# PV runs of 12, 10 and 10 units on twelve score buffers in a gated mix of attention and SwiGLU

## The chip, the cores and the metric

The kernel runs on one core of a Trainium2 chip. The metric is device time in microseconds (us). TensorE (PE in the profile) multiplies matrices, ScalarE (ACT) computes the exponentials, VectorE (DVE) and GpSimd (POOL) work on tiles in SBUF, and SyncE (SP) issues the DMAs, one after the other in the order of the program. The kernel is written with a manual schedule: each engine executes its instructions in the order in which the program emits them and waits where an operand is not ready.

## The reference

```python
q, k, v = split(x @ wqkv)                  # S = 2048, D = 512, 32 heads of 16
p = softmax(einsum("bhqd,bhkd->bhqk", q, k) * 16 ** -0.5)
a = einsum("bhqk,bhkd->bhqd", p, v) @ wo
h = silu(x @ w1) * (x @ w3)                # F = 1792
b = h @ w2
g = sigmoid((x * gate_w).sum(-1))
out = g * a + (1 - g) * b
```

All data are float32. The kernel splits the operands of the projections and the FFN in two parts (`hi` and `lo`) and sums three products, to keep the precision.

## The kernel before

After a preamble of some 80 us (transposes of x, the first heads' q and k, v, the gate) one string of tokens, `order`, drives everything else. A **unit** is one block of scores: two heads, 128 keys, 512 queries, so that a step (one pair of heads and one half of the queries) has 32 units, and there are 1024 units in 32 steps. The tokens are:

- **Q**, `score` (L823): one unit's scores, two matmuls on the two halves of the array's rows (L829), and one exp on ScalarE (L833) from PSUM (`S`, two buffers) into one of the score buffers `p` in SBUF.
- **F**, `feed` (L765): one matmul on each half of the rows for work that has nothing to do with the current scores. Two lanes take blocks from `blocks` (L716) in turn: first the q and k projections of the other heads (24 blocks), then the FFN's gate and up products (both `w_product`, L432), then the products of h with w2 (`h_product`, L550), then the output projection. A block of 12 such feeds runs on one half of the rows, then on the other, and its bank `f` (three of them) is then read by VectorE. A new block may take a bank only `REST` = 7 tokens after this.
- **P**, `pv` (L813): the products of two units' exps with V, eight matmuls (L817) that add into `acc`. It frees two score buffers.

Before, `one` has eight units, 21 feeds and one run of four P, and stands 90 times. `two` has eight units, 15 feeds and two runs of two P, and stands 37 times. Eight score buffers, `p0` to `p7`, hold the units between their Q and their P.

What a Q triggers besides: at unit 6 of each step `load_step` (L285) issues 14 DMAs with the next step's `Qt` and `Kt`; deferred work is taken from lists, one item per unit or so: `splits` (GpSimd's halves of weights), `soon` (a gate's exp, at the last Q ahead of a P), `small` (the reciprocals and products of the gates on VectorE, L461 to L481), `loads` (the w2 rows and pieces of h, `halves_of` L508), `stages` (the division by the sums, `divide` L605).

What a finished block triggers (`done`): a q or k block is copied to `gs` (L443), split on GpSimd into `sg` and `gs` (L444, L445) and stored (L187); `gs` and `sg` have two buffers each. A gate is copied (L455), an up product multiplied (L477), and the product with the sigmoid (L481) stored to `h_d` (L482). Pieces of h come back by `load_piece` (L522, load L512), are cast on GpSimd to the high half (L513) and subtracted for the low half (L514). The last P of a step calls `evac` (L795): VectorE copies `acc` to `u` (L799), and SyncE stores it with eight DMAs (L805, L811).

So VectorE, GpSimd and SyncE have a queue of their own in the order of the tokens, and a token that is moved takes what it triggers along.

Of the kernel before, what the change touches and what calls it, by code (L numbers as in the profile page):

```python
# [8 lines left out]
F32 = mybir.dt.float32  # L9
# [8 lines left out]
P = 128  # L18
S = 2048
D = 512  # L20
F = 1792
# [12 lines left out]
def gated_mix_kernel(ctx: ExitStack, tc: tile.TileContext, x, wqkv, wo, w1, w3, w2, gate_w, out):  # L34
# [47 lines left out]
    def slot(tag, dtype=F32R, shape=(P, 512)):  # L82

        return (fw if tag[0] == "f" else fk).tile(list(shape), dtype, name=tag, bufs=BUFS.get(tag, 2))

    def psum2():
        return psum.tile([P, 2, 512], F32, name="S", bufs=2)
# [237 lines left out]
    splits, issued, fed = [], 0, 0  # L325
# [91 lines left out]
    wk = ctx.enter_context(tc.tile_pool(name="wk", bufs=1))  # L417
# [116 lines left out]
    def load_wo(k):  # L534
        if k < 2:
            hi, lo = w2H[3][:, 2 + k, :], w2L[3][:, 2 + k, :]
        else:
            both = wk.tile([P, 2, 512], F32R, name=f"wo{k}")
            hi, lo = both[:, 0, :], both[:, 1, :]
        halves_of(wo[P * k:P * k + P, :], hi, lo, "sg")  # L540
        wo_[k] = hi, lo

    PART = NF
    y_ = {}
# [17 lines left out]
    def h_done(t, part):  # L562
        def done(ps):
            if part == 0:
                y_[t] = wk.tile([P, 512], F32, name=f"y{t % 2}")
                nc.vector.tensor_scalar(y_[t], ps, omg[:, t:t + 1], None, op0=OP.mult)
                return
            y = y_[t]
            nc.vector.scalar_tensor_tensor(y, ps, omg[:, t:t + 1], y, op0=OP.mult, op1=OP.add)
            if part == 1:  # L570
                return
            nc.sync.dma_start(B_d[P * t:P * t + P, :], y)
            if t in (11, 12, 13):
                load_bt(t - 11)
            if t in (4, 5, 6, 7):
                later.append(lambda: load_wo((0, 1, 3, 2)[t - 4]))
            if t == NT - 1:
                stages.append(rest_of_o())
        return done
# [10 lines left out]
    def reciprocals(k, half):  # L590

        rows = lambda d: d[8 * k:8 * k + 8, 1024 * half:1024 * half + 1024].rearrange("h (a t) -> h a t", a=16)
        nc.sync.dma_start(dd, rows(D_d))
        for _ in range(9):
            yield
        nc.vector.reciprocal(dd, dd)
        yield
        nc.sync.dma_start(rows(R_d), dd)

    def fetch_o(k, b, o, r):  # L600
        nc.sync.dma_start(o, O_d[P * k:P * k + P, 512 * b:512 * b + 512])
        src = R_d[8 * k:8 * k + 8, 512 * b:512 * b + 512]
        nc.sync.dma_start(r, bass.AP(tensor=src.tensor, offset=src.offset, ap=[[S, 8], [0, DH], [1, 512]]))

    def divide(k, half):  # L605

        yield from reciprocals(k, half)
        for b in (2 * half, 2 * half + 1):
            for _ in range(5):
                yield  # L610
            if half == 0:
                o, r = slot("hx", F32), slot("gw", F32)
            else:
                both = wk.tile([P, 2, 512], F32, name="od")
                o, r = both[:, 0, :], both[:, 1, :]
            fetch_o(k, b, o, r)
            for _ in range(7):
                yield
            nc.gpsimd.tensor_mul(o, o, r)
            for _ in range(3):  # L620
                yield
            nc.sync.dma_start(N_d[P * k:P * k + P, 512 * b:512 * b + 512], o)
            yield

    bt = {}

    def load_bt(t):
        bt[t] = wk.tile([P, 512], F32, name=f"bt{t % 3}")
        nc.sync.dma_start(bt[t], B_d[P * t:P * t + P, :])

    def o_product(t):
# [25 lines left out]
    def o_done(t):  # L657
        def done(ps):
            mix(t, ps)
            if t < 2:  # L660
                load_ot(t + 6)
            if t < 5:
                load_bt(t + 3)
        return done
# [8 lines left out]
    def rest_of_o():  # L673
        for n, x in zip("HL", (Oh, Ol)):
            for m in range(2):
                both = xp.tile([P, 4, 512], F32R, name=f"x{n}{m}")
                x[2 * m], x[2 * m + 1] = both[:, 0:2, :], both[:, 2:4, :]
        for m, n in enumerate("HL"):
            rows = xp.tile([P, 4, 512], F32, name=f"x{n}2")
            for i in range(4):  # L680
                bt[NT // 2 + 4 * m + i] = rows[:, i, :]
        for k in range(ND - 1):
            for b in (2, 3):
                halves_of(N_d[P * k:P * k + P, 512 * b:512 * b + 512], Oh[k][:, b - 2, :], Ol[k][:, b - 2, :], "fr")
                for _ in range(4):
                    yield
        for t in range(NT // 2, NT):
            nc.sync.dma_start(bt[t], B_d[P * t:P * t + P, :])
            yield
# [105 lines left out]
    def evac(j, half):  # L795
        if half == 1 and j == NPAIR - 1:
            return
        u = wk.tile([P, 512], F32, name="u")
        nc.vector.tensor_copy(u, acc)  # L799
        for gq in range(2):  # L800
            t = 1024 * half + 512 * gq
            for h in range(2):
                r = 32 * (2 * gq + h)
                hh = 2 * j + h
                nc.sync.dma_start(D_d[hh:hh + 1, t:t + 512], u[r + DH:r + DH + 1, :])  # L805
        for gq in range(2):
            t = 1024 * half + 512 * gq
            for h in range(2):
                r = 32 * (2 * gq + h)
                hh = 2 * j + h  # L810
                nc.sync.dma_start(O_d[DH * hh:DH * hh + DH, t:t + 512], u[r:r + DH, :])  # L811

    def pv(two):  # L813
        for j, half, k, gq, n, p in two:
            for h in range(2):
                r = 32 * (2 * gq + h)
                nc.tensor.matmul(acc[r:r + DH + 1, :], V[:, k, 2 * j + h, :], p[:, h, :],  # L817
                                 start=k == 0, stop=k == NT - 1)
            free.append(n)
        if k == NT - 1:  # L820
            evac(j, half)

    def score(j, half, k, gq):  # L823
        i = (NPAIR * half + j) % 2
        ps = psum2()
        t = 512 * gq
        for h in range(2):
            r = 64 * h
            nc.tensor.matmul(ps[:, h, :], Kt[i][r:r + 50, P * k:P * k + P],  # L829
                             Qt[i][r:r + 50, t:t + 512], start=True, stop=True)  # L830
        n = free.pop(0)
        p = wk.tile([P, 2, 512], F32, name=f"p{n}")
        nc.scalar.activation(p, ps, AF.Exp, scale=SCALE)  # L833
        return j, half, k, gq, n, p

# [2 lines left out]


    NP = 8  # L840
    LONG, SHORT = 90, 37
    one = "QQFFFFFF" + "QFFF" * 5 + "QPPPP"
    two = "QFFF" * 5 + "QPPQQPP"
    order = one * LONG + "QQ" + "F" * 7 + two * SHORT + "QFFF" * 5 + "QPPPP"
    free = list(range(NP))

    units = iter([(j, half, k, gq) for half in range(2) for j in range(NPAIR) for k in range(NT) for gq in range(2)])
    pend, clock = [], 0
    for i, c in enumerate(order):
        clock += 1 if c != "P" else 4  # L850
        if c == "Q":
            step = issued // 32 + 1
            if issued % 32 == 6 and step < 2 * NPAIR:
                assert 8 * (ND - 1) - qk_left >= 8 * min(step // 4, ND - 1)
                load_step(step)
            pend.append(score(*next(units)))
            issued += 1
            while splits and splits[0][0] <= issued:
                splits.pop(0)[1]()
            while soon and order[i + 1] == "P":  # L860
                soon.pop(0)()
            if issued % 128 == (40 if issued // 128 == 5 else 12) and 1 <= issued // 128 < 8:
                stages.append(divide((issued // 128 - 1) % 4, (issued // 128 - 1) // 4))
            if issued == 64 * NPAIR - 22:
                stages.append(six_heads())
            if small or later and hurry:
                for _ in range(3 if hurry else 1 + (len(small) > (6 if len(over) < 8 * len(chunks) - 16 else 0))):
                    if small or later and hurry:
                        (small or later).pop(0)()
            if loads and (hurry or issued % 2 or len(over) > 8 * len(chunks) - 12):  # L870
                loads.pop(0)()
            for stage in stages[:1]:
                if next(stage, stages) is stages:
                    stages.pop(0)
        elif c == "F":
            feed()
        else:
            pv(pend[:2])
            pend = pend[2:]
# [20 lines left out]
    k = ND - 1  # L900
# [80 lines left out]
```

## Time and profile before

| | us |
|---|---|
| runs of the kernel | 1403.93, 1404.1, 1404.19 |
| median | 1404.1 |
| the profiled execution | 1403.71 |
| its span in the profile | 1401.9 |
| TensorE busy | 1393.8 |
| ScalarE busy | 1034.3 |
| VectorE busy | 486.9 |
| GpSimd busy | 329.3 |
| mean granted clock | 0.999 |

The span is what the hardware profiler saw from the first instruction to the last; the execution takes 1.8 us more around it. In a row of the timeline stand the start, the duration, the engine, the line of the kernel, the operation, the tiles written and read, and the number of instructions that the row joins; in brackets comes the idle time of the engine before it and what ended it. Rows of TensorE overlap a little, since the next matmul starts while the last one drains. PEld is the loading of weights, which runs beside the matmuls, and SPq is the issuing of DMAs by SyncE.

### The profile page before, as it was taken

The page shows a single profiled execution, that of the slowest core. Times are in us where ns is not written, and L with a number is a line of the kernel's source. Part 1 is how long each engine was busy: PE and PEld are TensorE (multiplying, and loading weights), DVE is VectorE, ACT ScalarE, POOL GpSimd, SP SyncE. Part 2 cuts the span into 40 slices and gives each one's busy share as a digit, 9 for nine tenths or more (in the row PEclk, how much of TensorE's full clock was granted, in tenths as well). Part 3 has the DMA queues.
Part 4 walks back from the last instruction along what each step waited for, and adds up shares of the span by engine and source line. Part 5 has one row for each costly group of instructions (what it writes and reads, how often), then busy time and mean ns, then how long its engine had stood idle before and what let it go on. Part 6 is the DMA issues. An engine that isn't in the chain of part 4 may idle for free.

```text
span 1401.9 us, 29019 instructions
## 1 busy us (share of the span) xinstructions
PE 1393.8 (99%) x11497; PEld 826.4 (59%) x11497; DVE 486.9 (35%) x1083; ACT 1034.3 (74%) x1155; POOL 329.3 (23%) x366
## 2 busy tenths in 40 slices
PE   9999999999999999999999999999999999999998
PEld 8866566566566566566566566566555555555554
DVE  5511111564555546555454554511111101111113
ACT  4457677777777777777777777777677887888784
POOL 6123433011011101110110116432344322212312
PEclk9999999999999999999999999999999999999999
DMA  7653554343223423223333236444354453444632
GB/s 209 166 124 94 133 139 113 73 113 77 46 56 85 114 54 76 69 66 93 74 77 74 66 86 165 118 95 91 87 123 105 105 110 77 111 93 110 157 120 78
DMA packets 112479, 141.03 MB, mean 101 GB/s; under 512 B 16276, under 2 KB 70804, under 8 KB 109264
## 3 DMA queue, kind: packets, MB, share of 16 engines
q1 hardware_dynamic: 111616, 137.92, 41.4%
q8 instruction: 93, 1.52, 0.5%
q10 hardware_dynamic: 720, 1.18, 0.2%
q14 instruction: 50, 0.41, 0.1%
HBM read 90.43 MB, written 48.61 MB: 99 GB/s over the span
## 4 chain that ended last, share of the span: by engine, by line
PE 99%; DVE 0%; issue 0%; DVEq 0%
PE acc L817 33%; PE f L432 27%; PE S L829 19%; PE f L550 11%; PE f L634 2%; PE S L199 2%; PE f L641 1%; PE f L96 1%; PE f L98 1%; PE f L97 1%; PE f L165 0%; PE acc L353 0%; PE f L897 0%; PE S L165 0%; PE S L897 0%; DVE xL L646 0%
## 5 line engine op out<-in xcount | busy, mean ns | idle before, releaser
L833 ACT ACTIVATE p<-S 128x1024 f32<-128x1024 f32 x1024 | 967.9, 1026 | 314.1 <-PE S L829 305.0
L817 PE MATMUL acc<-p,V 128*17 128x512 f32 x4096 | 471.5, 594 | 0.0
L829 PE MATMUL S<-Qt,Kt 50*128 50x512 f32 x2048 | 403.7, 407 | 0.8 <-DVE V L415 0.8
L829 PEld LDWEIGHTS S<-Qt,Kt 50*128 50x128 f32 x2048 | 184.0, 184 | 173.5 <-issue 77.7
L817 PEld LDWEIGHTS acc<-p,V 128*17 128x17 f32 x4096 | 103.4, 97 | 275.2 <-issue 275.2
L463 DVE RECIPROCAL sg<-sg 128x64 f32<-128x64 f32 x448 | 209.2, 517 | 52.7 <-issue 49.1
L432 PE MATMUL f<-xH,fl 64*128 64x512 f32 x1088 | 220.6, 395 | 0.0
L432 PE MATMUL f<-xL,fh 64*128 64x512 f32 x1088 | 219.6, 393 | 0.0
L432 PE MATMUL f<-xH,fh 64*128 64x512 f32 x1088 | 218.0, 389 | 0.0
L328 POOL CAST fh<-fr 128x512 fp32r<-128x512 f32 x34 | 22.4, 658 | 428.0 <-DMA fr<-in_B_w_dram 279.6
L432 PEld LDWEIGHTS f<-xH,fh 64*128 64x128 f32 x1088 | 105.6, 184 | 25.0 <-issue 0.4
L432 PEld LDWEIGHTS f<-xL,fh 64*128 64x128 f32 x1088 | 106.4, 186 | 22.5
L432 PEld LDWEIGHTS f<-xH,fl 64*128 64x128 f32 x1088 | 106.1, 186 | 22.7
L789 DVE MEMSET tick<- 1x1 f32 x198 | 11.7, 59 | 281.2 <-PE f L550 143.0
L455 DVE COPY gs<-f 128x512 f32<-128x512 f32 x56 | 38.5, 688 | 65.5 <-PE f L432 59.3
L461 DVE TENSOR_SCALAR sg<-sg 128x512 f32<-128x512 f32 x56 | 27.3, 488 | 88.0 <-ACT sg L460 84.3
L550 PE MATMUL f<-xH,fh 64*128 64x512 f32 x208 | 57.5, 392 | 0.0
L550 PE MATMUL f<-xH,raw 64*128 64x512 f32 x192 | 57.0, 392 | 0.0
L550 PE MATMUL f<-xL,fh 64*128 64x512 f32 x208 | 56.2, 392 | 0.0
L550 PE MATMUL f<-xH,fl 64*128 64x512 f32 x208 | 55.4, 392 | 0.0
L513 POOL CAST fh<-sg 128x512 fp32r<-128x512 f32 (+1 forms) x32 | 18.0, 563 | 147.3 <-DMA sg<-h_d 91.0
L799 DVE COPY u<-acc 128x512 f32<-128x512 f32 x31 | 21.4, 692 | 86.1 <-PE acc L817 86.1
(202 smaller groups left out, 1324.6 us busy)
## 6 DMA issues: line engine op xcount, KB each, us to landing
Kt<-kH_d SPq DMA_DIRECT2D x128, 128.0 KB
h_d<-sg SPq DMA_DIRECT2D x56, 256.0 KB
sg<-h_d SPq DMA_DIRECT2D x43, 256.0 KB
fr<-in_B_w_dram SPq DMA_DIRECT2D x42, 256.0 KB
Qt<-qH_d SPq DMA_DIRECT2D x128, 64.0 KB
Kt<-kL_d SPq DMA_DIRECT2D x64, 128.0 KB
Qt<-qL_d SPq DMA_DIRECT2D x64, 64.0 KB
b_d<-y SPq DMA_DIRECT2D x16, 256.0 KB
```

The costliest lines, as they stand in the source:

```text
L199: nc.tensor.matmul(ps[:, i, :], w[i][h][:, k, :], xs[b][:, k, :], start=n == 0, stop=n == len(order) - 1)
L328: nc.gpsimd.tensor_copy(hi, src)
L432: return nc.tensor.matmul(ps, w[i == 1][r, k, :], (xL if i == 2 else xH)[b][r, k, :], start=n == 0 and not second, stop=n == 3 * ND - 1 an ...
L455: nc.vector.tensor_copy(gs, ps)
L461: small.append(lambda: nc.vector.tensor_scalar(sg, sg, 1.0, None, op0=OP.add))
L463: small.append(lambda q=q: nc.vector.reciprocal(sg[:, q:q + 64], sg[:, q:q + 64]))
L550: ins = nc.tensor.matmul(ps, hs[t][q][i == 1][r, P * o:P * o + P], (w2L if i == 2 else w2H)[q][r, o, :], start=n == 0 and not second, stop ...
L634: return nc.tensor.matmul(ps, ot[t][i == 1][r, P * k:P * k + P], wo_[k][i == 2][r, :], start=n == 0 and not second, stop=n == 3 * ND - 1 a ...
L799: nc.vector.tensor_copy(u, acc)
L817: nc.tensor.matmul(acc[r:r + DH + 1, :], V[:, k, 2 * j + h, :], p[:, h, :], start=k == 0, stop=k == NT - 1)
L829: nc.tensor.matmul(ps[:, h, :], Kt[i][r:r + 50, P * k:P * k + P], Qt[i][r:r + 50, t:t + 512], start=True, stop=True)
L833: nc.scalar.activation(p, ps, AF.Exp, scale=SCALE)
```

## The change

In the first 16 steps (512 units) the string has, for each step, one run of 12 units and two of 10, in place of four of eight. A run has six feeds after its first two scores and three after each further one up to the last, so a step holds 87 feeds where it had 84. After these come 18 periods of eight units and 45 of the double kind. The numbers of Q, F and P are the same in all; there are 157 runs of P where there were 165.

Twelve units must be held between Q and P. The four further buffers are tiles that are used only later: `od`, `yy` (the two `y` tiles joined in one) and the two halves of a tile `bt` (`b0`, `b1`, called `twin`), which replaces the three `bt` tiles. After 512 units they are not given back to `free`. The last `divide` of the first half reads into `od` where it took `hx` and `gw`.

```diff
     def h_done(t, part):
         def done(ps):
             if part == 0:
-                y_[t] = wk.tile([P, 512], F32, name=f"y{t % 2}")
+                if t == 0:
+                    y_[-1] = wk.tile([P, 2, 512], F32, name="yy")
+                y_[t] = y_[-1][:, t % 2, :]
...
-            if half == 0:
+            if half == 0 and k < 3:
                 o, r = slot("hx", F32), slot("gw", F32)
...
     def load_bt(t):
-        bt[t] = wk.tile([P, 512], F32, name=f"bt{t % 3}")
+        if t == 0:
+            bt[-1] = wk.tile([P, 4, 512], F32, name="bt")
+        bt[t] = bt[-1][:, t % 3, :]
...
-            free.append(n)
+            if type(n) is int or issued < 32 * THIRDS:
+                free.append(n)
...
         n = free.pop(0)
-        p = wk.tile([P, 2, 512], F32, name=f"p{n}")
+        if n in ("b0", "b1"):
+            p = twin[:, 0:2, :] if n == "b0" else twin[:, 2:4, :]
+        else:
+            p = wk.tile([P, 2, 512], F32, name=f"p{n}" if type(n) is int else n)
...
-    LONG, SHORT = 90, 37
-    one = "QQFFFFFF" + "QFFF" * 5 + "QPPPP"
+    THIRDS, LONG, SHORT = 16, 18, 45
+    run = lambda n: "QQFFFFFF" + "QFFF" * (n - 3) + "Q" + "P" * (n // 2)
     two = "QFFF" * 5 + "QPPQQPP"
-    order = one * LONG + "QQ" + "F" * 7 + two * SHORT + "QFFF" * 5 + "QPPPP"
-    free = list(range(NP))
+    order = (run(12) + run(10) * 2) * THIRDS + run(8) * LONG + "QQ" + "F" * 7 + two * SHORT + "QFFF" * 5 + "QPPPP"
+    MORE = ["od", "yy", "b0", "b1"]
+    free = list(range(NP)) + MORE
+    twin = wk.tile([P, 4, 512], F32, name="bt")
```

In the changed kernel the lines from L568 on have other numbers: the score matmuls are L834, PV is L821, the copy of acc L803, its stores L809 and L815.

Three places show what moves. The first is on TensorE at the end of the first step. `xH_157` with `fl` and `fh` of the second weight chunk is the first product of a new q or k block; the P run of unit 32 is `acc<-...`. Before, the rows read:

```order
L829 MATMUL S<-Qt_108,Kt_111 128x512 [waits Activation_49]
L829 MATMUL S<-Qt_108,Kt_111 128x512
L817 MATMUL acc<-p_6190,V 17x512 x2
L817 MATMUL acc<-p_6195,V 17x512 x2
...
L829 MATMUL S<-Qt_109,Kt_112 128x512 [waits PE_49]
L829 MATMUL S<-Qt_109,Kt_112 128x512
L432 MATMUL f<-xH_157,fl_6033 128x512 [waits DVE_49]
L432 MATMUL f<-xH_586,fl_653 128x512
```

After the change, at the same place:

```order
L834 MATMUL S<-Qt_108,Kt_111 128x512 [waits Activation_49]
L834 MATMUL S<-Qt_108,Kt_111 128x512
L432 MATMUL f<-xH_157,fl_6041 128x512 [waits DVE_49,Pool_49]
L432 MATMUL f<-xH_586,fl_653 128x512
L432 MATMUL f<-xL_158,fh_6040 128x512
L432 MATMUL f<-xL_587,fh_652 128x512
L432 MATMUL f<-xH_157,fh_6040 128x512
L432 MATMUL f<-xH_586,fh_652 128x512
L834 MATMUL S<-Qt_108,Kt_111 128x512 [waits Activation_49]
L834 MATMUL S<-Qt_108,Kt_111 128x512
L821 MATMUL acc<-bt,V 17x512 x4
L821 MATMUL acc<-p_6195,V 17x512 x2
```

The matmul that waits for VectorE's copy of a bank stood behind the run of P and stands ahead of it now.

The second place is on VectorE at the end of the fifth step (unit 160), around the copy of acc. Before:

```order
L461 TENSOR_SCALAR sg<-sg 128x512
L463 RECIPROCAL sg<-sg 128x64
L799 COPY u<-acc 128x512
L463 RECIPROCAL sg<-sg 128x64 x3
L477 TENSOR_TENSOR raw<-f,gs 128x512
L463 RECIPROCAL sg<-sg 128x64 x2
L455 COPY gs<-f 128x512
```

After:

```order
L455 COPY gs<-f 128x512
L463 RECIPROCAL sg<-sg 128x64 x3
L803 COPY u<-acc 128x512
L481 TENSOR_TENSOR sg<-raw,sg 128x512
L461 TENSOR_SCALAR sg<-sg 128x512
L463 RECIPROCAL sg<-sg 128x64 x2
L477 TENSOR_TENSOR raw<-f,gs 128x512
L463 RECIPROCAL sg<-sg 128x64 x2
```

Two full-width operations of a gate and two reciprocals now stand between the copy of acc and L477, the operation that reads a bank of TensorE; three reciprocals did before.

The third place is on SyncE, where the FFN ends and the products of h begin. L482 stores h, L512 with `h_d` loads a piece of it, and L277, L270 and L282 are the 14 DMAs of `load_step`. Before, behind those 14:

```order
L282 DMA Qt_108<-m_d 2x1024 x2
L512 DMA fr<-h_d 128x4x128
L482 DMA h_d<-sg 128x512
L512 DMA fr<-h_d 128x2x128
L512 DMA fr<-in_B_w_dram 128x512 x2
L512 DMA sg<-h_d 128x4x128
L482 DMA h_d<-sg 128x512
L512 DMA sg<-h_d 128x4x128
L512 DMA sg<-h_d 128x2x128
L512 DMA sg<-h_d 128x4x128
```

After:

```order
L512 DMA sg<-h_d 128x4x128
L482 DMA h_d<-sg 128x512
L512 DMA sg<-h_d 128x4x128
L277 DMA Qt_108<-qH_d 16x1024
L277 DMA Qt_108<-qL_d 16x1024
...
L270 DMA Kt_111<-kL_d 16x2048
L282 DMA Qt_108<-m_d 2x1024 x2
L512 DMA sg<-h_d 128x4x128
L512 DMA sg<-h_d 128x2x128
L512 DMA sg<-h_d 128x4x128
```

The last store of h and the first load behind it were followed by the further loads of h; the 14 DMAs of a step now lie between.

## The prediction

> **What bounds the kernel now.** I read the page first.
>
> ```profile
> PE 1393.8 (99%) x11497; PEld 826.4 (59%) x11497; DVE 486.9 (35%) x1083; ACT 1034.3 (74%) x1155; POOL 329.3 (23%) x366
> ...
> PE 99%; DVE 0%; issue 0%; DVEq 0%
> PE acc L817 33%; PE f L432 27%; PE S L829 19%; PE f L550 11%; PE f L634 2%; PE S L199 2%; PE f L641 1%; PE f L96 1%; PE f L98 1%; PE f L97 1%; PE f L165 0%; PE acc L353 0%; PE f L897 0%; PE S L165 0%; PE S L897 0%; DVE xL L646 0%
> ...
> L833 ACT ACTIVATE p<-S 128x1024 f32<-128x1024 f32 x1024 | 967.9, 1026 | 314.1 <-PE S L829 305.0
> ```
>
> TensorE is busy for 1393.8 of 1401.9 us and carries 99% of the chain that ended last. So a saving exists only if TensorE's own stream gets shorter, and any wait that TensorE gets is lost in full. The waits of TensorE come next.
>
> ```profile
> PE acc L353 <- DVE acc L349: 1.6, 1, 1.6
> PE S L829 <- DVE V L415: 0.8, 1, 0.8
> ```
>
> Both lie ahead of the token string: the list has no wait in the string itself. Third, the timeline of TensorE over one long period (eight units, one P run) and one short one (eight units, two P runs):
>
> ```profile
> 602.68 3.63 PE L817 MATMUL acc<-p,V 128*17 128x512 f32 x32
> 606.24 0.73 PE L829 MATMUL S<-Qt,Kt 50*128 50x512 f32 x4
> ...
> 608.22 0.40 PE L829 MATMUL S<-Qt,Kt 50*128 50x512 f32 x2
> ...
> 612.86 0.39 PE L829 MATMUL S<-Qt,Kt 50*128 50x512 f32 x2
> 613.18 0.62 PE L817 MATMUL acc<-p,V 128*17 128x512 f32 x4
> ```
>
> ```profile
> 1203.63 1.91 PE L817 MATMUL acc<-p,V 128*17 128x512 f32 x16
> 1205.47 0.73 PE L829 MATMUL S<-Qt,Kt 50*128 50x512 f32 x4
> ...
> 1213.04 0.62 PE L817 MATMUL acc<-p,V 128*17 128x512 f32 x4
> ```
>
> The long period is 613.18 − 602.68 = 10.50 us, the short one 9.41. Between 608.22 and 612.86 lie five groups QFFF: 4.64 / 5 = 0.928 each, so 0.232 for a token Q or F. A run of eight units' PV takes 3.56 (602.68 to 606.24), one of four 1.84: the difference is 0.43 per unit, and 0.12 is left over for the run. A unit in a run of any length n therefore adds 0.928 + 0.43 = 1.358: run(n) = 10.50 + (n − 8) × 1.358.
>
> **The change: the P runs.** The matmuls are the same 1024 Q, 2467 F and 512 P before and after; only the number of P runs changes, 165 to 157. A step of 32 units with its 87 feeds costs 15.93 + 2 × 13.22 = 42.37 us. So the string is 16 × 42.37 + 18 × 10.50 + 45 × 9.42 = 1290.8 against 90 × 10.50 + 37 × 9.42 = 1293.5; with the periods' means over all repeats (10.504 and 9.419) the difference is **−2.9 us**. That is 0.36 for each of eight P runs fewer: the change of direction between Q or F and P, which is all that the change can gain.
>
> Does a run of 12 starve somewhere? ScalarE must deliver an exp for each Q:
>
> ```profile
> 606.84 7.54 ACT L833 ACTIVATE p<-S 128x1024 f32<-128x1024 f32 x8 [1.93 <-PE S L829]
> ```
>
> Eight exps, the last 1.026 long, in 7.54: a pitch of (7.54 − 1.026) / 7 = 0.93, the pitch of QFFF itself. ScalarE follows the scores and does not fall behind with n; I take 0 (bounds 0 to 0.1 per run of 10 or 12, 5 us over 48 runs, if its own pitch were above 0.93). The four new score buffers add no instruction and no DMA. The last divide of the first half writes another tile, with the same instructions: 0.
>
> **The change: what loses its cover.** A P run is also 3.4 to 5.1 us in which VectorE, GpSimd and SyncE catch up while TensorE needs nothing of them. Longer stretches of Q and F lie between P runs now. Three places, by the order of the changed kernel and rows of before.
>
> *The q/k projections (first three steps).* Each finished bank is copied (L443), split on GpSimd and stored; the third copy needs the buffer that the store of the first one frees.
>
> ```profile
> 113.62 0.69 DVE L443 COPY gs<-f 128x512 f32<-128x512 f32 x1 [5.60 <-issue]
> ...
> 115.07 1.30 POOL L445 TENSOR_TENSOR gs<-gs,sg 128x512 f32<-128x512 f32 x1
> ...
> 116.39 0.32 SPq L187 DMA_DIRECT2D kL_d<-gs  x1
> ...
> 118.87 0.69 DVE L443 COPY gs<-f 128x512 f32<-128x512 f32 x1 [2.46 <-DMA kL_d<-gs]
> ...
> 119.50 1.91 PE L817 MATMUL acc<-p,V 128*17 128x512 f32 x16
> ```
>
> From the first copy's start to the third's end: 118.87 + 0.69 − 113.62 = 5.94. The last matmul of a block starts 0.4 before its copy and TensorE resumes 0.15 after one ends: 6.5 in all. Before, a P run starts there (119.50) and hides it. At unit 31 of the changed string the dependent matmul stands 20 F and 7 Q after the first block's last matmul, and ahead of the P run: 27 × 0.232 = 6.26, a wait of 0.25. At units 78 to 84 it is 20 F and 6 Q, 6.03: a wait of 0.5. Together **+0.75** (0 to 2; two more such places would make 2).
>
> *Gate work behind the copy of acc at a step's end.* The trace has one stall of this kind, in the period from 791.78 to 802.71, 0.43 longer than its neighbours:
>
> ```profile
> 795.47 0.69 DVE L799 COPY u<-acc 128x512 f32<-128x512 f32 x1 [0.91 <-PE acc L817]
> 796.08 1.78 DVE L463 RECIPROCAL sg<-sg 128x64 f32<-128x64 f32 x4
> 797.77 0.63 DVE L477 TENSOR_TENSOR raw<-f,gs 128x512 f32<-128x512 f32 x1
> ...
> 800.33 0.68 DVE L455 COPY gs<-f 128x512 f32<-128x512 f32 x1
> ```
>
> ```profile
> 800.82 0.81 PE L432 MATMUL f<-xH,fh 64*128 64x512 f32 x2
> 801.16 0.70 PE L829 MATMUL S<-Qt,Kt 50*128 50x512 f32 x2
> ```
>
> The copy of acc waits for the whole P run, and what is queued behind it on VectorE waits too; TensorE's pause ends 0.15 after the copy at 800.33 does. In the changed order, at unit 160, the copy of acc is followed by two full-width operations, two reciprocals (0.42 each) and L477 (0.69): 0.61 + 0.61 + 0.5 + 0.85 + 0.69 = 3.26. The copy starts 3.69 + 0.86 = 4.55 after a five-pair run begins, so the bank is free at 4.55 + 3.26 + 0.15 = 7.96; TensorE wants it after 4.42 of PV, QQ, 9 F and 2 Q: 4.42 + 0.58 + 11 × 0.232 = 7.55. A wait of 0.4. For some four step ends with such a queue I take 1.0 (0 to 2.5), less the 0.43 of before, which moves away: **+0.6**.
>
> *The start of the h products.* By unit 512 the changed string has issued 48 feeds more, so the FFN ends some 18 units earlier; the fetching of the next step's Qt and Kt (14 DMAs on SyncE's queue, at unit 6 of each step) stays at its unit. Thus it now stands between the last store of h and the loads of h that the products need.
>
> ```profile
> 876.21 3.63 PE L817 MATMUL acc<-p,V 128*17 128x512 f32 x32
> ...
> 881.80 1.69 SPq L811 DMA_DIRECT2D o_d<-u  x4
> ...
> 883.59 0.37 SPq L512 DMA_DIRECT2D fr<-in_B_w_dram  x1
> ...
> 884.77 0.38 SPq L277 DMA_DIRECT2D Qt<-qH_d  x1
> ...
> 892.29 0.39 SPq L512 DMA_DIRECT2D fr<-h_d  x1
> ...
> 897.51 0.61 POOL L513 CAST fh<-fr 128x512 fp32r<-128x512 f32 x1 [9.16 <-DMA fr<-h_d]
> ...
> 906.73 0.33 SPq L482 DMA_DIRECT2D h_d<-sg  x1
> ...
> 909.04 0.37 SPq L512 DMA_DIRECT2D sg<-h_d  x1
> ```
>
> Count from the start X of the P run that ends unit 608. SyncE is through the stores of u at +7.38 (883.59 − 876.21); two w2 loads, an h load and the h store bring +8.8; the load that reads the stored h issues 2.31 later (909.04 − 906.73), +11.1, and takes 0.4. Then come the 14 DMAs: 7.5 here (884.77 to 892.29), 6.8 one step earlier (846.81 to 853.57, below). The next h load issues at +18.3 to +19.0. A load that follows these 14 lands late: 892.29 to 897.51 is 5.2; 853.57 to 858.99 is 5.4; as bounds I take 4 and 6. Its cast takes 0.61, TensorE starts 0.15 later: +23.1 to +25.8, with 24.7 in the middle.
>
> ```profile
> 846.81 0.91 SPq L277 DMA_DIRECT2D Qt<-qH_d  x1
> ...
> 853.57 0.38 SPq L512 DMA_DIRECT2D fr<-h_d  x1
> ...
> 858.99 0.61 POOL L513 CAST wo<-fr 128x512 fp32r<-128x512 f32 x1 [6.07 <-DMA fr<-h_d]
> ```
>
> TensorE wants it at the next P run plus 19 F and 7 Q: 10.50 + 3.56 + 0.58 + 24 × 0.232 = +20.2. That is a wait of 4.5 (2.9 to 5.6). One feed later it wants the low half, which GpSimd writes for 1.3 after the cast: another 1.1. Together **+5.6** (4.0 to 6.7; 0 if the load finds itself ahead of the 14 DMAs).
>
> **Sum.** −2.9 + 0.75 + 0.6 + 5.6 = +4.05. The profiled execution took 1403.71 and would take 1407.8; the median of the three runs is 1404.1, so I predict **1408.1 us**. What a measurement of this kernel can tell from no change is 0.2%, 2.8 us: below 1401.3 is faster, above 1406.9 slower.
>
> **The clock gate.** A wait of 4.5 us raises a question that the trace answers only at the end, where TensorE has no work left after 1396.12:
>
> ```profile
> 1396.00:1397.00 1.00, 0.12 (x1) 0.00 (x0) 1.00 (x3) 0.00 (x0) 0.00 (x0) 1.00 1.02 381
> ...
> 1398.00:1399.00 1.00, 0.00 (x0) 0.00 (x0) 0.00 (x0) 0.00 (x0) 0.00 (x0) 0.81 1.01 377
> 1399.00:1400.00 1.00, 0.00 (x0) 0.00 (x0) 0.00 (x0) 0.00 (x0) 0.00 (x0) 0.50 0.73 260
> ```
>
> In these windows the column before the last two is the granted clock: 1.00 in the first, 0.81 in the third microsecond, then 0.50. So it fell to half some 2.5 us after the last matmul, and a wait of 4.5 us may bring the same in the middle. How long the half clock then lasts no row shows; half a clock for about as long as the wait would cost 2 us more. The Trainium skill ("TensorE: Matmul & The Clock Gate", section "Part 1: The HAM clock gate (the "warmup" mystery)") speaks against this change in the same way: after an idle window of about 3.4 us the array runs at half rate until it has been busy for about as long. By that rule the loss would be an estimated 1.7 us and the time 1409.8; the trace agrees that the clock halves, though here after 2.5 us.
>
> **Rivals.**
> 1. *Every wait is covered* (chance 0.10): −2.9 − 0.43, 1401.0 us, faster. For it: the list of waits has none in the string, and the trace's one stall is 0.43. Against it: 20 F and 7 Q are less than the 6.5 that a row chain measures, and SyncE's queue is strictly in order.
> 2. *The h load is ready in time, the small waits stay* (0.18): −2.9 + 0.75 + 0.6 = −1.55, 1402.6 us. It needs the 14 DMAs and the landing together in some 8 us in place of 12 to 13, against both rows of landing.
> 3. *The clock falls too* (0.20): the forecast and 2 us, 1410.1. For it the windows above; against it that the wait may be shorter than 2.5.
> 4. *ScalarE becomes the bound in the long runs* (0.04): 0.1 for each of 48 runs, with the waits 1412.9. Against it the pitch of 0.93 and the 305 us in which ScalarE waits for scores.
>
> My forecast has 0.48. The decisive point between it and the second rival is one number: the start of the cast behind the 14 DMAs, against +20.2.
>
> **Chances and range.** Faster: rival 1's larger part, 0.07. Slower: rivals 3 and 4 and most of the forecast, whose own range is 1406.0 to 1410.0: 0.59. Same: the rest, 0.34. The range from 1402.2 to 1410.8 takes in rival 2, rival 3 and the bounds of the h wait, and leaves out rivals 1 and 4 and the worst sums.
>
> **What would show it.** In the profile after: 48 P runs in the first 16 steps, with 13.22 us from run to run in the tens and 15.93 in the twelves; the waits of TensorE with a new line on L550 for GpSimd, 3 to 7 us, near 900 us; waits on L432 for VectorE, under 0.6 each, near units 31, 84 and 160; the h load's issue behind the 14 DMAs of Qt and Kt, and its cast 5 us or more later. I am wrong if L550 has no wait, if a run's period is off by over 0.05, or if the granted clock falls below 1.00.

## The result and the profile after

| | before | after |
|---|---|---|
| median, us | 1403.93 (5 runs) | 1420.29 (5 runs) |
| profiled execution, us | 1403.71 | 1420.64 |
| its span, us | 1401.9 | 1418.8 |
| TensorE busy, us | 1393.8 | 1398.6 |
| mean granted clock | 0.999 | 0.994 |

The change costs 16.4 us: the ratio is 1.0116, with a 95% interval from 1.0105 to 1.0128. The direction was forecast, the size was not: +4 was predicted, in a range up to 1410.8.

The page of the profile after, TensorE's busy time and the chain that ended last:

```profile
PE 1398.6 (99%) x11497; PEld 835.1 (59%) x11497; DVE 483.9 (34%) x1083; ACT 1034.0 (73%) x1155; POOL 327.8 (23%) x366
...
PE 88%; issue 4%; DMA 2%; POOL 2%; SPq 1%; DVE 1%; ACT 1%; DVEq 0%; POOLq 0%; ACTq 0%
```

TensorE's share of the chain fell from 99% to 88%, and DMA, GpSimd, SyncE's queue and ScalarE have joined it: TensorE now waits for them. It is also busy for 4.8 us longer, though it does the same work with fewer changes of direction, so there is something besides waiting. The waits of TensorE after:

```profile
PE S L834 <- ACT p L841: 5.4, 2, 5.1
PE f L550 <- POOL fr L513: 5.4, 1, 5.4
PE acc L353 <- DVE acc L349: 1.6, 1, 1.6
PE S L834 <- DVE V L415: 0.7, 1, 0.7
PE f L550 <- POOL fr L514: 0.6, 1, 0.6
```

Two waits of over 5 us are new. The second is the forecast one at the start of the h products. The first stands in no step of the prediction.

The long runs themselves take what was computed. Starts of a run of 12, of the two of 10 behind it and of the next 12, from TensorE's timeline:

```profile
602.68 3.63 PE L821 MATMUL acc<-p,V 128*17 128x512 f32 x32
...
616.73 0.62 PE L821 MATMUL acc<-p,V 128*17 128x512 f32 x4
...
629.96 0.62 PE L821 MATMUL acc<-bt,V 128*17 128x512 f32 x4
...
645.05 0.61 PE L821 MATMUL acc<-od,V 128*17 128x512 f32 x2
```

From 602.68 to 645.05 is 42.37 us, the computed value of a step to the last digit; the saving of 2.9 is there. (The single distances are 14.05, 13.23 and 15.09: from start to start one counts the run of P just begun and the units that come behind it, so the forecast 15.93 and 13.22 show only in the sum of a step.) (The counts at the ends of these rows are cut by the window and by the buffers' names; a run of 12 units has 48 of them.)

**The first stall, near 769 us.** It is in the step that begins at unit 512. SyncE's queue, VectorE, ScalarE and TensorE in one window of the timeline:

```profile
766.15 0.36 SPq L277 DMA_DIRECT2D Qt<-qH_d  x1
...
768.63 0.69 DVE L481 TENSOR_TENSOR sg<-raw,sg 128x512 f32<-128x512 f32 x1
...
770.39 0.62 ACT L460 ACTIVATE sg<-gs 128x512 f32<-128x512 f32 x1
...
772.62 0.58 SPq L282 DMA_DIRECT2D Qt<-m_d  x2
...
773.30 10.16 SPq L482 DMA_DIRECT2D h_d<-sg  x2
...
778.51 0.63 ACT L460 ACTIVATE sg<-gs 128x512 f32<-128x512 f32 x1 [7.50 <-DMA h_d<-sg]
779.05 2.98 ACT L841 ACTIVATE p<-S 128x1024 f32<-128x1024 f32 x3
780.11 0.79 PE L834 MATMUL S<-Qt,Kt 50*128 50x512 f32 x2 [5.12 <-ACT p L841]
```

The 14 DMAs of the next step run from 766.15 to 773.2. The store of h, whose data VectorE (L481) had ready at 769.3, issues behind them, at 773.30, and the exp that waits for it starts 5.2 us later. At the end of the run that ends at unit 520 two gates' exps were pending. The second one (L460) writes the `sg` buffer that this store reads, so ScalarE stands for 7.5 us. Its queue is in order, so the exps of the scores behind it stand too; `S` has two buffers, and TensorE stops for 5.1 us. Before, two gate exps also stood side by side at the end of a run in eight places, and the second never waited; the one of unit 512:

```profile
750.86 1.14 ACT L460 ACTIVATE sg<-gs 128x512 f32<-128x512 f32 x2
```

After, four of ten such pairs wait, for 3.4, 2.8, 4.4 and 7.5 us. The run of P covers most of the first three.

**The second stall, near 913 us,** is the forecast one. SyncE, GpSimd and TensorE:

```profile
901.24 0.45 SPq L482 DMA_DIRECT2D h_d<-sg  x1
905.42 0.37 SPq L512 DMA_DIRECT2D sg<-h_d  x1
905.88 0.45 SPq L277 DMA_DIRECT2D Qt<-qH_d  x1
...
913.49 7.83 SPq L512 DMA_DIRECT2D sg<-h_d  x4
...
917.82 0.61 POOL L513 CAST fr<-sg 128x512 fp32r<-128x512 f32 x1 [6.77 <-DMA sg<-h_d]
...
918.49 0.79 PE L550 MATMUL f<-xH,fr 64*128 64x512 f32 x1 [5.39 <-POOL fr L513]
...
920.99 5.58 PE L821 MATMUL acc<-p,V 128*17 128x512 f32 x32
```

The first of the four further loads of h stands behind the 14 DMAs; its cast starts 4.3 us after its issue. The run of PV after it takes 5.58 in place of 3.63 us and waits for nothing. The windows say why (span and length of the window; busy us of TensorE, of its loading of weights, of VectorE, ScalarE and GpSimd; the granted clock; share and GB/s of the DMA engines):

```profile
774.50:778.00 3.50, 0.49 (x6) 0.05 (x2) 0.79 (x2) 0.00 (x0) 0.00 (x0) 1.00 0.68 117
778.50:780.00 1.50, 0.00 (x0) 0.00 (x0) 0.00 (x0) 1.49 (x3) 0.00 (x0) 0.50 0.00 0
780.00:785.00 5.00, 4.89 (x24) 3.85 (x26) 2.13 (x5) 3.60 (x5) 0.00 (x0) 0.50 0.14 53
785.50:787.00 1.50, 1.50 (x16) 1.29 (x14) 1.50 (x5) 1.26 (x2) 0.00 (x0) 1.00 0.05 11
913.20:918.00 4.80, 0.00 (x0) 0.00 (x0) 0.00 (x0) 0.80 (x1) 0.18 (x1) 1.00 0.76 120
918.50:924.50 6.00, 5.45 (x26) 1.56 (x30) 0.00 (x0) 1.02 (x1) 4.04 (x5) 0.50 0.22 66
925.00:928.00 3.00, 3.00 (x28) 1.45 (x22) 0.06 (x1) 0.90 (x1) 0.76 (x2) 1.00 0.00 0
```

After both waits TensorE works at half clock, until 785.0 and until 925.0. So each long wait costs about half as much again.

The account, by the time from P run to P run against the computed one: fewer runs −2.9; the first stall +7.63 (18.13 against 10.50: 5.1 of wait, 2.5 of half clock); the second +9.28 (7.28 in its period and 2.00 in the next: 6.0 of wait, 3.3 of half clock); eight small waits +3.3; the stall of before gone −0.43. The sum is +16.9, as the spans have it.

### The profile page after: what moved, and what is told of

Same layout as the page of the kernel before. It is cut to its first block, busy times and chain, and to the rows that moved or that the text cites. A ratio compares the mean times of both kernels' runs of the same rounds, so it can differ in the third digit from the quotient of the medians.

```text
span 1418.8 us, 29039 instructions
## 1 busy us (share of the span) xinstructions
PE 1398.6 (99%) x11497; PEld 835.1 (59%) x11497; DVE 483.9 (34%) x1083; ACT 1034.0 (73%) x1155; POOL 327.8 (23%) x366
## 4 chain that ended last, share of the span: by engine, by line
PE 88%; issue 4%; DMA 2%; POOL 2%; SPq 1%; DVE 1%; ACT 1%; DVEq 0%; POOLq 0%; ACTq 0%
PE acc L821 30%; PE f L432 22%; PE S L834 17%; PE f L550 11%; PE f L638 2%; PE S L199 2%; PE f L645 1%; PE f L96 1%; PE f L98 1%; PE f L97 1%; DMA kH_d<-sg 1%; POOL gs L445 1%; DMA h_d<-sg 1%; SPq L270 1%; ACT p L841 1%
## 5 line engine op out<-in xcount | busy, mean ns | idle before, releaser
L841 ACT ACTIVATE p<-S 128x1024 f32<-128x1024 f32 x854 | 810.3, 1026 | 251.1 <-PE S L834 242.0
L834 PE MATMUL S<-Qt,Kt 50*128 50x512 f32 x2048 | 410.3, 407 | 6.1 <-ACT p L841 5.4
L821 PE MATMUL acc<-p,V 128*17 128x512 f32 x3416 | 401.5, 596 | 0.0
L834 PEld LDWEIGHTS S<-Qt,Kt 50*128 50x128 f32 x2048 | 188.3, 185 | 172.9 <-ACT p L841 82.8
L432 PE MATMUL f<-xH,fl 64*128 64x512 f32 x1088 | 224.3, 397 | 0.5 <-DVE tick L793 0.3
L821 PEld LDWEIGHTS acc<-p,V 128*17 128x17 f32 x3416 | 86.2, 97 | 231.1 <-issue 231.1
L432 PE MATMUL f<-xH,fh 64*128 64x512 f32 x1088 | 221.4, 390 | 0.3 <-DVE gs L455 0.3
L841 ACT ACTIVATE bt<-S 128x1024 f32<-128x1024 f32 x84 | 82.2, 1028 | 20.3 <-PE S L834 20.3
L841 ACT ACTIVATE od<-S 128x1024 f32<-128x1024 f32 x43 | 44.3, 1029 | 41.4 <-PE S L834 41.4
L550 PE MATMUL f<-xH,fh 64*128 64x512 f32 x208 | 58.3, 394 | 0.0
L550 PE MATMUL f<-xH,fr 64*128 64x512 f32 x160 | 52.0, 397 | 5.9 <-POOL fr L513 5.4
L550 PE MATMUL f<-xH,raw 64*128 64x512 f32 x192 | 57.7, 392 | 0.0
L803 DVE COPY u<-acc 128x512 f32<-128x512 f32 x31 | 21.4, 692 | 104.6 <-PE acc L821 97.1
L550 PE MATMUL f<-xL,fh 64*128 64x512 f32 x208 | 56.1, 392 | 0.0
```

What stands on the lines that cost most here:

```text
L432: return nc.tensor.matmul(ps, w[i == 1][r, k, :], (xL if i == 2 else xH)[b][r, k, :], start=n == 0 and not second, stop=n == 3 * ND - 1 an ...
L550: ins = nc.tensor.matmul(ps, hs[t][q][i == 1][r, P * o:P * o + P], (w2L if i == 2 else w2H)[q][r, o, :], start=n == 0 and not second, stop ...
```

## The experiments

The theory to test: both stalls come from the **place of 14 DMAs** on SyncE's queue relative to a store or load of h, not from the length of the runs as such and not from the new buffers; the half clock adds to their price. Before's median in these comparisons is 1403.7 to 1403.9.

**One or both groups of 14 DMAs moved.** In three kernels a single line of the changed kernel differs. The entry 17 moves the DMAs of unit 518 to 526, the entry 20 those of unit 614 to 626; e1 has only the first, e2 only the second:

```diff
-            if issued % 32 == 6 and step < 2 * NPAIR:
+            if issued % 32 == {17: 14, 20: 18}.get(step, 6) and step < 2 * NPAIR:
```

> The changed kernel with one edit: the 14 DMAs of the step at unit 518 are issued at unit 526. Queue theory (at unit 518 the 14 DMAs stand on SyncE's queue ahead of a store of h, ScalarE's gate exp waits for that store, and the score exps queue behind it): the wait of 5.1 us on the scores and the half clock after it go, 7.6 us in all, so 1420.3 becomes about 1412.7. Rival (ScalarE waits because two gates' exps are taken at the end of one run and need both sg buffers, whatever SyncE does): a wait of 3 us or more on the scores stays near unit 522, time within 3 us of 1420.3.

> The changed kernel with one edit: the 14 DMAs of the step at unit 614 are issued at unit 626. Queue theory: the load of h issues some 7 us earlier and lands in about 3 us; the wait on L550 for GpSimd falls from 6.0 us to 0 to 2.5, below the length at which the clock halves, so the P run of 5.5 us is one of 3.56 again: 9.3 becomes 0 to 2.5, 1420.3 becomes 1411 to 1413.5. Rival (store, load and cast of h are late by themselves, since the FFN ends earlier): the wait stays above 4 us and the clock still falls, time within 2 us of 1420.3.

> Both edits, units 518 to 526 and 614 to 626. Queue theory: the sum, 14.4 to 16.9 less than 1420.3, so 1403.4 to 1405.9, and a granted clock of 1.00 through the whole string; what is left is the small waits (3.3) against the saved switches (2.9). Rival (the waits only move on to the next place where a queue is late): less than 12 of the 16.9 us come back, above 1408.

Measured: e1 1412.4 (ratio to before 1.0059, 1.0042 to 1.0076), e2 1412.1 (1.0063, 1.0046 to 1.0080), e3 1404.6 (1.0007, 0.9997 to 1.0017). All three are in the range of the queue theory, and 15.7 of the 16.4 us are gone with both. In e1, ScalarE's second gate exp waits 0.77 instead of 7.50:

```profile
772.74 0.63 ACT L460 ACTIVATE sg<-gs 128x512 f32<-128x512 f32 x1 [0.77 <-DMA h_d<-sg]
```

In e2 the cast that was at 917.82 starts at 911.67, and the waits of TensorE no longer list L550:

```profile
911.67 0.61 POOL L513 CAST fr<-sg 128x512 fp32r<-128x512 f32 x1 [0.97 <-DMA sg<-h_d]
```

e3 is no faster than before: the eight fewer changes of direction are worth less than the small waits that came.

**The buffers alone.** The changed kernel with the order string of before:

```diff
-    order = (run(12) + run(10) * 2) * THIRDS + run(8) * LONG + "QQ" + "F" * 7 + two * SHORT + ...
+    order = run(8) * 90 + "QQ" + "F" * 7 + two * 37 + ...
```

> The changed kernel with the order string of before (90 periods of eight units, 37 double ones): the twelve score buffers, the joined tiles and the divide that reads into od stay. Queue theory: none of these costs anything, 1403.9 within 1. Rival (buffers that are reused as h or divide tiles bring the waits): above 1407.

Measured: 1403.55, ratio 0.9999 (0.9989 to 1.0008). Twelve buffers, the joined tiles and the moved divide cost nothing.

**Only one gate exp at the end of that run.** e2 (the DMAs of unit 518 in place) with:

```diff
             while soon and order[i + 1] == "P":
                 soon.pop(0)()
+                if issued == 520:
+                    break
```

> e2_step20 (the DMAs of unit 518 still at 518) with one edit: at the end of the run that ends at unit 520 only one of the two pending gate exps is taken, the other at the end of the next run. Theory with two conditions (two gate exps at one run's end, which need both sg buffers, and the 14 DMAs ahead of the store that frees the second): the 7.8 us near 769 us go without any DMA being moved, 1412.1 becomes 1404.6, unless the second exp's delay makes the banks late, then up to 2 more. Rival (the 14 DMAs delay something else that TensorE needs, and the exps only show it): a wait of 4 us or more stays, 1409 or above.

Measured: 1404.4, ratio 1.0005 (0.9996 to 1.0015). The stall goes though the DMAs of unit 518 stay where they are. ScalarE in this run:

```profile
770.16 0.62 ACT L460 ACTIVATE sg<-gs 128x512 f32<-128x512 f32 x1
773.23 7.55 ACT L841 ACTIVATE p<-S 128x1024 f32<-128x1024 f32 x8 [2.45 <-PE S L834]
780.67 0.62 ACT L460 ACTIVATE sg<-gs 128x512 f32<-128x512 f32 x1
```

The second exp now stands at the end of the next run, at 780.67, and waits for nothing. So the first stall needs both: two gate exps at one run's end, and the 14 DMAs ahead of the store that frees the second one's buffer. Pairs of gate exps stood at the ends of runs before, too; the new string brought one of them together with a store behind the 14 DMAs.

**How much of the 14 DMAs it takes.** With the DMAs of unit 518 moved, those of unit 614 were split: e8 leaves the six of `Qt` ahead of the loads of h and moves the eight of `Kt` and the guard to unit 627; e9 leaves three of `Kt` too.

```diff
-                load_step(step)
+                (load_q(step % NPAIR, step // NPAIR, step % 2) if step == 20 else load_step(step))
...
+            if issued == 627:
+                load_k(20 % NPAIR, 0)
+                load_guard(20 % NPAIR, 20 // NPAIR, 0)
```

> The changed kernel with the DMAs of unit 518 at 526, and of those of unit 614 only the eight of Kt and the guard moved (to unit 627); the six of Qt stay ahead of the loads of h. Queue theory: the wait on L550 grows with the number of DMAs ahead: some 0.4 with none (e2_step20), 7.3 with 14 (the changed kernel, without the half clock behind it), so 2.5 to 4 with six; if it stays under about 3 us the clock does not fall and the time is 1404.6 + 2 to 3.5. Rival (only Kt's big transfers matter, through the landing and not through the queue): no more than 1 us of wait, 1404.6 to 1405.6.

Measured: 1404.9, ratio 1.0010 (1.0001 to 1.0019), a wait of 0.2 on L550: the rival's number, and the expectation was wrong. The reason is in the queue all the same. In e2 SyncE came to the load at 906.4, but the load must wait until GpSimd frees an `sg` buffer, at 908.7. In e8 the six issues fill this time:

```profile
898.88 0.45 SPq L277 DMA_DIRECT2D Qt<-qH_d  x1
...
901.69 5.31 SPq L512 DMA_DIRECT2D sg<-h_d  x3
...
904.64 0.61 POOL L513 CAST fr<-sg 128x512 fp32r<-128x512 f32 x1 [1.12 <-DMA sg<-h_d]
```

> As e8_half_moved (six DMAs of Qt ahead of the loads of h), with three of the six DMAs of Kt ahead too. Queue theory: in e2_step20 and e8_half_moved the load of h could not issue before GpSimd had freed an sg buffer, 2.8 us after SyncE came to it, and the six DMAs of Qt fitted into that time; each further DMA costs its 0.47 on SyncE, and a load behind Kt lands in some 4.3 instead of 3.0. So a wait of 1.4 + 1.3 = 2 to 3 us on L550 in place of 0.2, TensorE idle for too short a time to lose the clock: 1404.9 becomes 1406.5 to 1408. Rival (the clock falls after any wait over 2 us): 1408.5 or more, with windows of half clock.

Measured: 1408.8, ratio 1.0038 (1.0024 to 1.0052). The wait is in the range (2.2 and 0.6), the time is the rival's, by the clock. The waits and windows of e9 (its lines stand one lower, so L550 is L551 and L513 is L514):

```profile
PE f L551 <- POOL fr L514: 2.2, 1, 2.2
...
PE f L551 <- POOL fr L515: 0.6, 1, 0.6
```

```profile
906.50:908.00 1.50, 0.00 (x0) 0.00 (x0) 0.00 (x0) 0.86 (x1) 0.05 (x1) 1.00 0.49 122
908.50:915.00 6.50, 5.84 (x26) 1.62 (x30) 0.00 (x0) 1.02 (x1) 3.00 (x5) 0.50 0.62 113
915.50:917.00 1.50, 1.50 (x14) 0.40 (x8) 0.00 (x0) 0.00 (x0) 1.15 (x2) 1.00 0.08 11
```

Two waits of 2.7 us together cost 6.1 in the periods (4.04 and 2.04 over the computed ones): 3.4 of it is the half clock. This profiled execution is the slowest of the five (1408.1 to 1410.8) and has the lowest mean clock (0.997, the others 0.998 and 0.999), so in the others the half clock most likely cost less. Queue and landing both count: the load behind the three DMAs of `Kt` issues about 2 us later than in e8, and its cast starts 4.2 us after that in place of 3.0. A further kernel, with five of the six DMAs of `Kt` ahead, gave no result, so how the wait grows from there is open.

**The small waits.** e5 takes e3's place for unit 614, has the DMAs at unit 14 of every other step, and emits the copy of `acc` three units later in the first 16 steps, so that VectorE need not stand behind it:

```diff
-            if issued % 32 == 6 and step < 2 * NPAIR:
+            if issued % 32 == {20: 18}.get(step, 14) and step < 2 * NPAIR:
...
         if k == NT - 1:
-            evac(j, half)
+            if issued <= 512:
+                late.append((j, half))
+            else:
+                evac(j, half)
...
+            if late and issued % 32 == 3:
+                evac(*late.pop())
```

> The changed kernel with the 14 DMAs at unit 14 of each step (18 in step 19), and in the first 16 steps the copy of acc and its stores are emitted three units later, so that VectorE can do the gates' work during the run of P. Theory (the small waits at the step ends come from gate work queued behind a copy of acc that waits for the run of P): the waits near 347, 375, 560, 715 and 730 us of run e3_both, 2.0 us together, go; those of the q/k stage (105, 177 us, 1.0 together) stay; 1404.6 becomes about 1402.5. Rival (the waits come from longer stretches without P in general, so VectorE is late anyway): within 0.7 of 1404.6.

Measured: 1406.0, ratio 1.0017 (1.0008 to 1.0026), slower than e3. The six waits at step ends did go (2.4 us in e3's trace), but those of the q/k stage, three in each trace, grew from 1.5 to 3.4. The release of the third copy, in e3:

```profile
114.48 0.32 SPq L187 DMA_DIRECT2D kL_d<-gs  x1
...
116.93 0.69 DVE L443 COPY gs<-f 128x512 f32<-128x512 f32 x1 [2.45 <-POOL sg L444]
```

and in e5, where the 14 DMAs at unit 14 end at 112.15, just ahead of the q/k stores:

```profile
114.73 0.34 SPq L187 DMA_DIRECT2D kL_d<-gs  x1
...
118.24 0.69 DVE L443 COPY gs<-f 128x512 f32<-128x512 f32 x1 [3.50 <-DMA kL_d<-gs]
```

The copy starts 3.5 us after the store's issue in place of 2.45. (In e3 the row names GpSimd, so 2.45 is the most that the landing can have taken; in the prediction's rows of before, where the row names the store, it is 2.48.) So e12 put the DMAs back to unit 6 (as in e3) and began the late copy at step 5:

```diff
-            if issued <= 512:
+            if 128 < issued <= 512:
```

> e3_both (DMAs of unit 518 at 526, of 614 at 626, of every other step at unit 6) with the copy of acc emitted three units later in steps 5 to 16 only. Theory on the miss of e5_late_copy (its q/k waits grew from 1.5 to 3.4 us because the 14 DMAs at unit 14 stood in front of the q/k stores, whose landing went from 2.45 to 3.5): with the DMAs back at unit 6 the q/k waits are those of e3_both, and the waits at the step ends from step 5 on (2.5 us) go: 1404.6 becomes 1402.1 to 1402.6. Rival (the late copy itself delays the q/k stores or takes back its gain elsewhere): 1404 or above.

Measured: 1409.0, ratio 1.0042 (1.0027 to 1.0058); a miss again. The q/k waits are two of e3's (0.4 and 0.6), as the theory on e5's miss has it. But at three step ends where e3 loses 0.3, 0.8 and 0.6 us, e12 loses 3.7, 1.7 and 1.3. The first of them, on SyncE and ScalarE:

```profile
349.26 9.80 SPq L482 DMA_DIRECT2D h_d<-sg  x2
...
354.59 0.63 ACT L460 ACTIVATE sg<-gs 128x512 f32<-128x512 f32 x1 [5.98 <-DMA h_d<-sg]
```

The same two rows of e3:

```profile
347.81 9.74 SPq L482 DMA_DIRECT2D h_d<-sg  x2
...
353.06 0.63 ACT L460 ACTIVATE sg<-gs 128x512 f32<-128x512 f32 x1 [4.11 <-DMA h_d<-sg]
```

It is the first stall's mechanism. The eight stores of `u`, three units later, push the 14 DMAs behind them back, and the store of h behind those issues 1.45 later; of ScalarE's wait e3 hides nearly all under the run of PV, and e12 cannot. Here, too, half clock follows, though TensorE's wait is only 1.9 us:

```profile
356.18 0.49 PE L837 MATMUL S<-Qt,Kt 50*128 50x512 f32 x2 [1.88 <-ACT p L844]
```

```profile
353.94:357.35 3.41, 1.53 (x14) 0.93 (x12) 0.44 (x2) 2.76 (x4) 0.00 (x0) 1.00 0.00 1
357.35:360.76 3.41, 3.41 (x20) 2.65 (x18) 2.57 (x6) 2.54 (x3) 0.00 (x0) 0.50 0.22 82
```

e5 has the late copy at these three step ends as well, and there the second gate exp waits for nothing: at the first of them its store of h issues at 345.95, ahead of the 14 DMAs, which start at 346.42. At these ends e5 and e12 differ only in the place of the 14 DMAs. So it was that place which took these three waits away in e5, and the late copy alone makes them longer. The smaller losses at three other step ends (0.3, 0.1 and 0.3 in e3) are gone in both.

**Fewer long runs.** e6 has four steps in eights, eight steps of 12, 10 and 10, then 38 eights and 41 doubles; e7 the same with twelve (20 and 43). Both have the DMAs at unit 14 and the late copy everywhere.

```diff
-    order = (run(12) + run(10) * 2) * THIRDS + run(8) * LONG + "QQ" + ...
+    order = run(8) * 4 * FIRST + (run(12) + run(10) * 2) * THIRDS + run(8) * LONG + "QQ" + ...
```

> Four steps in runs of eight, then eight steps in runs of 12, 10 and 10, then eights (58 - 4 = 54 more periods minus those taken: 38) and 41 double periods; DMAs at unit 14, copy of acc three units late throughout. Theory: four P runs fewer save 1.45, the stall of 0.43 of before goes, no new wait: 1403.9 becomes about 1402.1. Rival (something waits at each long run that the list of waits hides): 1403.9 or above.

> As e6_four_eight, with twelve steps of 12, 10 and 10 in place of eight. Theory: six P runs fewer save 2.2, 0.43 goes, two or three small waits of 0.1 to 0.7 come: 1401.9 to 1402.5. Rival as there: 1403.9 or above.

Measured: e6 1401.7, ratio 0.9985 (0.9976 to 0.9994); e7 1402.6, ratio 0.9992 (0.9983 to 1.0001). e6 beats both kernels, by 0.15% against before; e7 is not told from before. In e6's trace no period of the string is over the computed one by more than 0.1 but one, by 0.41; e7 has two of 0.9.

Is that the runs or the other two edits? The kernel before with these edits alone:

> The kernel before with the two other edits of e6_four_eight and no longer runs: DMAs at unit 14, copy of acc three units later. Theory: before has one stall of 0.43 and nothing else to win, so 1403.3 to 1403.9, and the 2.0 us of e6_four_eight come from its four runs of P fewer (1.45) and the absence of that stall. Rival (e6's gain is the late copy's or the DMAs'): 1401.7 to 1402.3.

Measured: 1404.2, ratio 1.0005 (0.9996 to 1.0014), 0.3 over the expected range. The edits alone gain nothing, so e6's 2.0 us are the long runs': four fewer changes of direction at 0.36 make 1.45, and the rest is within the interval. In the profiled executions the string from the first run of P to the last takes 1292.9 us in e6 and 1294.5 before, which is 1.6 less; a stall of 0.41 stands where before has its 0.43, so that part of the expectation did not come true.

## Why the prediction failed

- *The saving.* Right: 42.37 us a step, −2.9, in the profile to 0.01; ScalarE keeps pace with runs of 12, so rival 4 is out.
- *The start of the h products.* Right in mechanism and nearly in size: 5.6 of wait forecast, 6.0 measured. Two parts of the working were off in opposite directions: the store that the first load reads took 4.2 (901.24 to 905.42), not 2.3, and the load behind the 14 DMAs landed in 4.3, not 5.3. That the sum came so close is in part luck.
- *The clock.* This was rival 3, and its mechanism held. I gave it 0.20 and 2 us; it took 3.3 there, and 2.5 at the other stall. It also needs less than the 2.5 us that I set against it: in e9 a first wait of 2.2 us was enough, in e12 one of 1.9.
- *The q/k stage and the step ends.* 1.8 forecast (0.75 and 1.0), 3.3 measured, in eight places. The two largest at step ends, 0.8 at 560 us and 0.6 at 730, I put to VectorE's queue. They stand where ScalarE's second gate exp waits 2.8 and 4.4 us for a store of h, and e12, which lets VectorE do the gate work first, makes them larger.
- **The step that failed** is the list "Three places, by the order of the changed kernel" as the full account of what loses its cover. It followed what stands behind the 14 DMAs only to the loads of h that TensorE needs through GpSimd. The same DMAs also stand ahead of a store of h, and what waits for that is a buffer, then an exp of a gate, then, in ScalarE's order, the scores. That is 7.6 of the 12.8 us by which the forecast falls short of the profile's account; the half clock of the h stall is 3.3, the small waits 1.5, the h wait itself 0.4. I had looked at ScalarE only for its pace; the 305 us in which it waits for scores seemed to prove slack, but an engine with a queue in order has none at the instant at which one of its instructions waits for a DMA.

## What to carry to other kernels

When a table of numbers moves compute, list for every DMA on the shared issuing queue what it is now ahead of, stores included, and follow each store through the buffer that it frees to the next writer and to what is queued behind that writer. The block of 14 DMAs was a wall of some 7 us here, and the place of such a block should be chosen after the new order is known, not kept at a count of units. Where the array can lose its clock, price a wait of about 2 us or more at its length and what the half clock adds, here 1.7 to 3.4 us; breaking one of the two long waits was worth more (7.6 or 9.3 us) than saving eight changes of direction (2.9).

## What the runs showed of the hardware

- The clock fell to 0.50 for 6.8 us at both long waits of the changed kernel, 778.2 to 785.0 and 918.2 to 925.0, and in e9, 908.5 to 915.3; in e12 it fell for 3.4 us, 357.4 to 360.8. The two falls of the changed kernel are 140.0 us apart, 41 times 3.41, which fits a fixed grid of windows.
- The time from TensorE's last matmul to the fall was 2.0 us in e9, 3.2 and 5.1 in the changed kernel, and in e12 TensorE had worked again for 1.2 us: the wait's length alone doesn't decide it. By that grid the window ahead of the fall was 42% busy in e9 (905.0 to 908.5) and 45% in e12 (353.9 to 357.4), and one with 52% (911.3 to 914.7 in the changed kernel) brought no fall. But one with 44%, at the end of e2 (1403.0 to 1406.4, other matmuls), brought none either, so the busy share alone doesn't decide it. The full clock came back after a window in which TensorE was busy throughout, the first one in e12 and the second one in the other three. The Trainium skill ("TensorE: Matmul & The Clock Gate", section "Part 1: The HAM clock gate (the "warmup" mystery)") has a free-running window of 3413 ns, and the trace agrees on that figure; it asks for an idle window, and here a window that was busy for 42% was enough, so the measurement goes further than the page. What the exact condition is, no run here shows.
- A store or load behind the 14 DMAs lands late: the store of q/k in 3.5 in place of 2.45 us at most (e5 against e3), the store of h in 5.2 in place of 2.4 (773.30 to 778.51 in the changed kernel, 770.30 to 772.74 in e1), the load of h in 4.3 in place of 3.0 (the changed kernel against e8). Each is taken from the issue to the start of what waits for it.
- DMAs on the queue cost nothing while the next one waits for a buffer anyway: six issues, 2.8 us, were free in e8.
